# Routing attention and a token/channel mixer on one core: the sums of exponentials taken from one half sum in 14 pairs, and the rounded channel weights stored in rows of 1792 bytes

## The chip, the core and the metric

The kernel runs on one core of a Trainium2 chip. Its engines work side by side and are ordered only by semaphores: TensorE multiplies matrices and writes to PSUM, VectorE and ScalarE do elementwise work and read PSUM, GpSimd does elementwise work between SBUF tiles and can issue transfers of its own, SyncE issues most of the transfers. In the profile they are called PE (PEld for its weight loads), DVE, ACT, POOL and SP. Sixteen DMA engines carry all transfers.

The metric is the time of one execution on the device in microseconds (us). Lower is better.

## What is computed

The inputs are in double precision. Per batch `b` and head `h` the reference gives each query and each key the cluster whose normalised centroid it fits best, and lets a query attend only to the keys of its own cluster. The heads put side by side are the input `x` of an MLP mixer with a token step and a channel step.

```python
q_assign = argmax(q_n @ c_n.T); k_assign = argmax(k_n @ c_n.T)   # 16 clusters per head
scores = where(q_assign == k_assign, q @ k.T / sqrt(64), -1e9)   # 768 x 768
attn = exp(scores - max); attn = attn / (sum(attn) + 1e-9)       # per query
x = concat over heads of attn @ v                                # (4, 768, 512)
u = x + (relu(x.T @ w_tok1) @ w_tok2).T                          # 768 -> 256 -> 768
out = u + relu(u @ w_ch1) @ w_ch2                                # 512 -> 1536 -> 512
```

There are 4 batches, 8 heads, 768 tokens and 64 channels per head.

## The kernel before

**Attention.** The 32 heads are worked as 16 pairs (`NP`), two heads at a time, by `pair(m)`. `scores(m)` issues 12 chunks of score products on TensorE, with a small second product that adds the mask, into PSUM banks 0 to 5 (chunk `n` uses banks `2*(n%3)` and the next one). ScalarE takes the exponential of each chunk (line 1191) into six buffers `st[0..5]` of `[128, 2, 768]`, out of a rotation of seven (`exs`). `values(m, i)` multiplies the exponentials with `v` (16 matmuls of 192 columns for each of `i` = 0 to 5, line 1208, into banks 6 and 7).

The divisor of the softmax needs the sum of the exponentials over all keys. VectorE first adds them elementwise: `es[0] = st[0]+st[1]+st[2]` and `es[1] = st[3]+st[4]+st[5]`, four additions of 128x1536 for a pair (line 881 is the helper `tt` that issues all of VectorE's and GpSimd's two-operand work). `sums(m, bk)` then multiplies both half sums with a matrix of ones, four matmuls of 384 columns for each half (also line 1208), into bank 5; this comes just ahead of `values(m, 5)`. `finish_x(m, 5)` is VectorE's closing part of a pair: transpose the sums (line 1250), clip them (1252), take the reciprocal (1259), transpose the values out of banks 6 and 7 into `x` (1264), and multiply (881). Inside the values of pair m lie the four matmuls of `route(m + 2, 0)`, whose result VectorE turns into cluster assignments (lines 1086 to 1091); the mask goes through DRAM (`wdm`) and back.

**Weights.** Beside attention, VectorE rounds the double precision weights to single precision in 31 pieces (`weight_round`, lines 1327 to 1337 and one addition), paced over the attention by planned times. For the channel weights, `channel_weights` loads pieces of two parts with rows of 512 bytes, writes four operands into `O`, forms four more by sums (`sub1`, 256 elements each), forms four combinations of seven operands (`sub2`, 448 elements each), and stores seven blocks per round to DRAM (`wd1`, `wd2`): 12 rounds, 84 stores of 224 KB with rows of 256 bytes.

**Token step and channel step.** Both use a seven-product scheme (sums of operands in place of an eighth product). In the channel step each of the 28 calls of `product` fetches seven blocks of weights of 192 KB from `wd1` or `wd2` into a ring of eight buffers (196 fetches with rows of 1536 bytes), one for three matmuls of 384 columns, and the results are taken out of PSUM by VectorE or ScalarE. In the products with `w_ch1` two sets of three PSUM banks take turns.

**What sets the order.** Every operation is added to a `Program` with its engine(s), a cost in the author's own figures, and what it reads and writes. `Program.plan` lays a schedule from these figures, TensorE in the order in which the work is written down, the others by due time, and the instructions are emitted in that order. On the chip each engine then runs its list in order and waits where a semaphore says so.

Of the kernel before, what the change touches and what calls it, by code (L numbers as in the profile page):

```python
# [9 lines left out]
F32 = mybir.dt.float32  # L10
# [10 lines left out]
P = 128  # L21
NJ = S // P
# [27 lines left out]
GRAIN = 32  # L50

# [668 lines left out]
def kernel(  # L720
# [36 lines left out]
    wd1 = dram.tile([7, 7, P, 3 * P], F32, name="wd1")  # L757
    wd2 = dram.tile([7, 7, P, 3, P], F32, name="wd2")
# [45 lines left out]
    O = buf(119, [8, 2, 2, W])  # L804
# [343 lines left out]
    def scores(m):  # L1148
# [26 lines left out]
        for n in range(2 * NJ):  # L1175
# [57 lines left out]
    def sums(m, bk):  # L1233
        for n in range(2):
# [4 lines left out]
                        tokens(es[n].ap.rearrange("p h t -> p (h t)"), gr), n == 0, n == 1,  # L1239
# [7 lines left out]
    def finish_x(m, bk):  # L1247
        b, hp = divmod(m, H // 2)
        x, rcp = xs[b], rcps[m % 2]
        vec(lambda: nc.vector.transpose(out=denT.ap, in_=ps[:, bk, 0:HS]), 0.57, bank(bk), denT.k())  # L1250
        def den():
# [9 lines left out]
        cols = slice(hp * P, (hp + 1) * P)  # L1261
        xk = x.rows(0, NJ, hp * P, (hp + 1) * P)
        vec(
            lambda: nc.vector.transpose(  # L1264
                out=x.ap[:, :, cols].rearrange("p j (c d) -> p c j d", d=32),
                in_=ps[:, 6:8, 0:HS],
            ),
            0.96, bank(6, 7), xk,
        )
# [13 lines left out]
    def pair(m):  # L1283
# [23 lines left out]
    def weight_round(srcs, dst, wr, perm=None, after=12.0):  # L1307
# [10 lines left out]
        for part, src, w in srcs:  # L1318
            dma(part(raw.ap), src, [], raw.k((2 * c, 2 * (c + w))), w, 512, after)
            c += w  # L1320
# [63 lines left out]
    def channel_weights(which, after):  # L1384
# [3 lines left out]
        for s in range(6):  # L1388
            for K in range(2):
                srcs = []  # L1390
                for kk in range(2):
                    def part(r, kk=kk):
                        r = r.rearrange("p (k c) two -> p k (c two)", k=2)
                        return r[:, kk].rearrange("p (m c) -> p m c", m=4)

                    kq = 2 * K + kk
                    if which == 1:
                        rows = slice(kq * P, (kq + 1) * P)
                        view = moe_w_ch1[rows].bitcast(U32).rearrange(
                            "p (m c) -> p m c", m=4  # L1400
                        )[:, :, 2 * W * s : 2 * W * (s + 1)]
                    else:
                        c, hf = divmod(s, 2)
                        rows = slice(kq * 3 * P + c * P, kq * 3 * P + (c + 1) * P)
# [602 lines left out]
```

## Time and profile before

| | before |
|---|---|
| median of 3 runs | 799.79 us (799.49 to 800.53) |
| the profiled execution | 799.38 us, of which its span is 797.6 us |
| granted TensorE clock | 0.999 |
| busy: TensorE, VectorE, ScalarE, GpSimd | 783.8, 659.4, 469.8, 188.8 us |
| attention, 16 pairs | up to 333 us of the span |
| token step | 333 to about 410 us |
| channel step | from about 409 us to the end |

The page's share of busy time is an average over stages. The windows of the profile give busy time in a stretch, the chain lists the work that ended last in order of time, and the groups by shape give the duration of one instruction. A busy TensorE says only that matmuls were under way. The column "DMA share" is the mean busy share of the 16 DMA engines; it can pass 1 because packets of one engine overlap.

### The profile page before, as it was taken

Reading aid. Unit: us, or ns where it says so; the run is one execution under the profiler, and the core shown is the slowest. Engines: PE = TensorE matmul, PEld = TensorE weight load, DVE = VectorE, ACT = ScalarE, POOL = GpSimd, SP = SyncE. Lnnn points to the kernel's source line nnn. Section 1 sums busy time; section 2 is a strip of 40 time slices with the busy share of each in tenths; the row PEclk is TensorE's granted clock in tenths of the full one; section 3 lists DMA queues with packets and bytes.
Section 4 is the critical chain, followed back from the end, with each engine's and each line's share of the span. In section 5 each row is a group of like instructions: output and inputs, shape, how many; then the busy total and the mean of one; then the engine's idle time right before and its main releaser. Section 6 shows DMA issues by size and latency. Waiting matters only on the chain.

```text
span 797.6 us, 15467 instructions
## 1 busy us (share of the span) xinstructions
PE 783.8 (98%) x6063; PEld 466.9 (59%) x6063; DVE 659.4 (83%) x861; ACT 469.8 (59%) x618; POOL 188.8 (24%) x184
## 2 busy tenths in 40 slices
PE   7999999999999999999999999999999999999997
PEld 5566666666666666544555555555555555555554
DVE  6988899999999999999994677899952566799964
ACT  5588888888888875698714568503256104400433
POOL 0000000000000000000353499800186379840000
PEclk9999999999999999999999999999999999999999
DMA  9466779999999985479848787635597433333766
GB/s 213 153 160 167 172 169 229 223 211 215 229 226 237 223 249 134 97 148 211 177 122 274 270 290 265 223 99 144 143 210 195 130 106 102 99 104 105 177 148 154
DMA packets 264881, 143.69 MB, mean 180 GB/s; under 512 B 184160, under 2 KB 260704, under 8 KB 264800
## 3 DMA queue, kind: packets, MB, share of 16 engines
q1 hardware_dynamic: 262432, 141.83, 70.2%
q8 instruction: 50, 0.82, 0.4%
q10 hardware_dynamic: 2368, 0.79, 0.4%
q14 instruction: 31, 0.25, 0.1%
HBM read 91.95 MB, written 28.61 MB: 151 GB/s over the span
## 4 chain that ended last, share of the span: by engine, by line
PE 82%; DVE 11%; ACT 4%; issue 2%; ACTq 0%; DVEq 0%
PE ps L842 65%; PE ps L1208 17%; DVE arena L881 9%; ACT arena L871 3%; ACT arena L861 1%; ACT arena L888 0%; DVE arena L863 0%; DVE arena L1264 0%; DVE arena L1337 0%; ACTq L901 0%; ACT L980 0%; ACT arena L1191 0%; DVE arena L1334 0%; DVE arena L1331 0%; DVE arena L1086 0%
## 5 line engine op out<-in xcount | busy, mean ns | idle before, releaser
L842 PE MATMUL ps<-arena 128*128 128x384 f32 (+5 forms) x2735 | 639.7, 462 | 8.4 <-DVE arena L881 2.1
L842 PEld LDWEIGHTS ps<-arena 128*128 128x128 f32 (+1 forms) x2351 | 341.1, 184 | 252.0 <-issue 62.7
L881 DVE TENSOR_TENSOR arena<-arena 128x1536 f32<-128x1536 f32 (+6 forms) x341 | 354.8, 1063 | 19.8 <-ACT arena L1191 9.0
L881 POOL TENSOR_TENSOR arena<-arena 128x384 f32<-128x384 f32 x178 | 188.1, 1086 | 516.5 <-DVE arena L881 382.4
L881 DVE TENSOR_TENSOR arena<-ps,arena 128x384 f32<-128x384 f32 (+3 forms) x227 | 189.3, 844 | 100.2 <-PE ps L842 90.4
L871 ACT COPY arena<-arena 128x768 uint16<-128x768 uint16 x223 | 192.0, 952 | 58.7 <-DVE arena L881 29.3
L1191 ACT ACTIVATE arena<-ps 128x768 f32<-128x768 f32 x192 | 153.8, 810 | 30.4 <-PE ps L842 29.3
L1208 PE MATMUL ps<-arena 128*32 128x192 f32 (+1 forms) x3328 | 151.1, 339 | 0.0
L1208 PEld LDWEIGHTS ps<-arena 128*32 128x32 f32 x3328 | 106.5, 110 | 48.0 <-issue 18.3
L861 ACT COPY arena<-ps 128x1152 f32<-128x1152 f32 (+2 forms) x45 | 32.8, 738 | 133.7 <-PE ps L842 125.2
L888 ACT ACTIVATE arena<-arena 128x1152 f32<-128x1152 f32 (+1 forms) x38 | 40.0, 1077 | 55.8 <-DVE arena L881 55.3
L1865 ACT ACTIVATE arena<-arena 128x768 f32<-128x768 f32 x40 | 38.5, 967 | 17.3 <-DMA arena<-in_moe_w_ch_dram 17.0
L842 PEld LDWEIGHTS <-arena 64*128 64x128 bf16 x384 | 19.2, 94 | 25.0 <-issue 0.6
L1095 ACT ACTIVATE arena<-arena 128x384 bf16<-128x384 f32 x16 | 11.3, 707 | 16.3 <-issue 9.9
L1331 DVE SCALAR_TENSOR_TENSOR arena<-arena 128x512 uint32<-128x512 uint32 (+1 forms) x31 | 20.5, 667 | 0.5
L1337 DVE SCALAR_TENSOR_TENSOR arena<-arena 128x512 f32<-128x512 uint32 (+1 forms) x31 | 20.3, 666 | 0.5
L1264 DVE STREAM_TRANSPOSE arena<-ps 128x768 f32<-128x768 f32 x16 | 15.6, 974 | 0.6 <-PE ps L1208 0.4
L1327 DVE TENSOR_SCALAR arena<-arena 128x512 uint32<-128x512 uint32 (+1 forms) x31 | 12.6, 406 | 0.3 <-DMA arena<-in_moe_w_ch_dram 0.3
L1334 DVE TENSOR_SCALAR arena<-arena 128x512 uint32<-128x512 uint32 (+1 forms) x31 | 12.3, 409 | 0.4
L1086 DVE STREAM_TRANSPOSE arena<-ps 128x384 f32<-128x384 f32 x16 | 9.2, 575 | 3.0 <-PE ps L842 2.7
L1250 DVE STREAM_TRANSPOSE arena<-ps 128x384 f32<-128x384 f32 x16 | 9.2, 575 | 0.8 <-PE ps L1208 0.6
L1091 DVE STREAM_TRANSPOSE arena<-arena 128x384 f32<-128x384 f32 x16 | 9.3, 578 | 0.6
(58 smaller groups left out, 47.2 us busy)
## 6 DMA issues: line engine op xcount, KB each, us to landing
arena<-wd SPq DMA_DIRECT2D x196, 192.0 KB, 2.4
wd<-arena SPq DMA_DIRECT2D x84, 224.0 KB, 3.6
arena<-in_moe_w_ch_dram SPq DMA_DIRECT2D x48, 256.0 KB, 4.6
arena<-in_moe_w_ch_dram SPq DMA_DIRECT2D x16, 768.0 KB, 5.3
arena<-in_v_dram SPq DMA_DIRECT2D x16, 384.0 KB, 4.8
out_dram<-arena SPq DMA_DIRECT2D x14, 384.0 KB, 4.1
arena<-in_k_dram SPq DMA_DIRECT2D x13, 384.0 KB, 4.0
arena<-in_q_dram SPq DMA_DIRECT2D x13, 384.0 KB, 4.4
```

Of the source, the lines that this page charges most:

```text
L842: nc.tensor.matmul(dst, lhsT=lhsT, rhs=rhs, start=start, stop=stop, tile_position=pos, is_transpose=tr, skip_group_check=True,)
L861: nc.scalar.copy(out=dst, in_=src)
L871: nc.scalar.copy(out=dst, in_=src)
L881: (nc.vector if e == "DVE" else nc.gpsimd).tensor_tensor(out=dst, in0=a, in1=b, op=op)
L888: nc.scalar.activation(out=dst, in_=src, func=ACT.Relu)
L1191: lambda e, ex=ex, s=s, u=u: nc.scalar.activation(out=ex.ap[:, :, u * HS : (u + 1) * HS], in_=ps[:, 2 * s : 2 * s + 2, 0:HS], func=ACT.Exp ...
L1208: nc.tensor.matmul(dst, lhsT=lhsT, rhs=rhs, start=start, stop=stop, tile_position=pos, skip_group_check=True,)
L1264: lambda: nc.vector.transpose(out=x.ap[:, :, cols].rearrange("p j (c d) -> p c j d", d=32), in_=ps[:, 6:8, 0:HS],),
L1327: vec(lambda: nc.vector.tensor_scalar(out=hh, in0=hi, scalar1=0x07FFFFFF, scalar2=3, op0=ALU.bitwise_and, op1=ALU.logical_shift_left,), f, ...
L1331: vec(lambda: nc.vector.scalar_tensor_tensor(out=TT, in0=hi, scalar=0xC0000000, in1=hh, op0=ALU.bitwise_and, op1=ALU.bitwise_or), 0.14 + 0 ...
L1337: vec(lambda: nc.vector.scalar_tensor_tensor(out=ll, in0=lo, scalar=float(2.0**-52), in1=hh.bitcast(F32), op0=ALU.mult, op1=ALU.mult,), 0. ...
L1865: lambda e, i=i, func=func, bias=bias, n=n, hi=hi: nc.scalar.activation(out=hi, in_=hi, func=func, bias=bias, accum_out=wsum.ap[:, i, n : ...
```

## The change

**Sums.** A string gives each of the 16 pairs a letter, `-VTVTVTVTVTVTVT-`. For the 14 pairs with a letter the second half sum takes in the first, and `sums` multiplies only `es[1]` with the ones (four matmuls in place of eight). For V (pairs 1, 3, ... 13) VectorE does the addition, one more of 128x1536. For T (pairs 2, 4, ... 14) GpSimd issues a transfer from `es[0]` to `es[1]` that adds at its destination (768 KB read, 768 KB added to). Pairs 0 and 15 keep both halves.

**Their place.** `sums(m - 1)` and the closing part that uses it now come after `values(m, 0)` of the next pair, still in bank 5; the additions of pair m are written down behind them. `finish_x` is split: the transpose of the values (part 0) stays at the end of its pair, the rest (part 1) goes with the sums. For pair 15 the sums stay ahead of `values(15, 5)`, in bank 4.

**Weights.** `wd1` and `wd2` become `wds`, stored as `[7, 128, 6, 7, 64]`: a store writes 1792 bytes in one row for each partition (128 rows in place of 896), and a fetch reads 256 bytes per row (768 rows in place of 128). `O` is laid out with the operand index inside, so that a store's source is contiguous, and a piece of weights is loaded by four transfers of 128 KB in place of two of 256 KB, with rows of 512 bytes as before.

```diff
+FOLD = "-VTVTVTVTVTVTVT-"
...
-    wd1 = dram.tile([7, 7, P, 3 * P], F32, name="wd1")
-    wd2 = dram.tile([7, 7, P, 3, P], F32, name="wd2")
+    wds = [dram.tile([7, P, 6, 7, W], F32, name=f"wd{i}") for i in (1, 2)]
...
-    O = buf(119, [8, 2, 2, W])
+    O = buf(119, [2, 2, 8, W])
...
+    def add_up(m):
+        st = unit[m]
         for n in range(2):
             a = es[n]
             x, y, z = st[HJ * n : HJ * n + HJ]
             tt(a.ap, x.ap, y.ap, ALU.add, 2 * S, x.k() + y.k(), a.k())
             tt(a.ap, a.ap, z.ap, ALU.add, 2 * S, a.k() + z.k(), a.k())
+        a, b = es[1], es[0]
+        if FOLD[m] == "V":
+            tt(a.ap, a.ap, b.ap, ALU.add, 2 * S, a.k() + b.k(), a.k())
+        if FOLD[m] != "T":
+            return
+
+        def fn(e):
+            nc.gpsimd.dma_start(
+                a.ap.rearrange("p h t -> p (h t)"), b.ap.rearrange("p h t -> p (h t)"),
+                accum_op=ALU.add,
+            )
+
+        g.add({"POOL": 1.0}, fn, a.k() + b.k(), a.k(), (2.2 * 768 * 1024, 6144))
...
     def sums(m, bk):
-        for n in range(2):
+        first = 0 if FOLD[m] == "-" else 1
+        for n in range(first, 2):
...
-                        tokens(es[n].ap.rearrange("p h t -> p (h t)"), gr), n == 0, n == 1,
+                        tokens(es[n].ap.rearrange("p h t -> p (h t)"), gr), n == first, n == 1,
...
-            if i == NJ - 1:
-                sums(m, 5)
+            if i == 1:
+                if m:
+                    sums(m - 1, 5)
+                    finish_x(m - 1, 5, 1)
+                add_up(m)
+            if i == NJ - 1 and m == NP - 1:
+                sums(m, 4)
             values(m, i)
-        finish_x(m, 5)
+        finish_x(m, 5, 0)
+        if m == NP - 1:
+            finish_x(m, 4, 1)
...
-                dma(d.rearrange("o p c -> p o c"), src, rd, [("wd", which, pn, s)],
-                    224, 4 * W)
+                dma(wds[which - 1][pn, :, s], src, rd, [("wd", which, pn, s)], 224, 28 * W)
...
-            src = wd1[qi, pn] if wide else wd2[qi, pn].rearrange("p a c -> p (a c)")
             dma(
-                w.ap.rearrange("p a c -> p (a c)"), src,
-                [("wd", which, pn, s) for s in range(6)], w.k(), 192, 1536,
+                w.ap.rearrange("p a (b c) -> p (a b) c", c=W), wds[which - 1][pn, :, :, qi],
+                [("wd", which, pn, s) for s in range(6)], w.k(), 192, 256,
             )
```

More of the change, by code (lines that the diff above doesn't have):

```diff
@@ L1317, in weight_round @@
         c = 0
-        for part, src, w in srcs:
-            dma(part(raw.ap), src, [], raw.k((2 * c, 2 * (c + w))), w, 512, after)
+        for part, src, w, *at in srcs:
+            dma(part(raw.ap), src, [], raw.k(*(at or [(2 * c, 2 * (c + w))])), w, 512, after)
             c += w
@@ L1391, in channel_weights @@
                 for kk in range(2):
[L1392 to L1394 removed]
                     kq = 2 * K + kk
                     if which == 1:
[L1398 to L1401, printed above, removed]
+                        w, at = moe_w_ch1[kq * P : (kq + 1) * P], 2 * W * s
```

67 lines of the change are left out of this document (35 added, 32 removed).

## The prediction

> **What bounds the kernel now.** I read the page's busy line first, then windows by stage, then the chain in order of time, then VectorE's groups by shape in the pairs' steady stretch.
>
> ```profile
> PE 783.8 (98%) x6063; PEld 466.9 (59%) x6063; DVE 659.4 (83%) x861; ACT 469.8 (59%) x618; POOL 188.8 (24%) x184
> ```
>
> ```profile
> 117.00:314.60 197.60, 197.60 (x2878) 123.45 (x2880) 190.58 (x276) 161.13 (x206) 0.00 (x0) 1.00 0.92 219
> ...
> 333.00:372.00 39.00, 38.43 (x93) 16.80 (x90) 34.97 (x59) 35.10 (x48) 0.00 (x0) 1.00 0.81 168
> 372.00:410.00 38.00, 36.49 (x109) 19.93 (x109) 37.16 (x75) 22.65 (x27) 13.31 (x13) 1.00 0.75 162
> ```
>
> ```profile
> 166.33 5.34 PE ps L1208 x128
> 171.66 0.65 PE ps L842 x8
> 172.31 3.89 PE ps L1208 x80
> 176.20 9.89 PE ps L842 x72
> ```
>
> The columns of the windows are length, then busy time of PE, PEld, DVE, ACT, POOL, then the granted clock, the DMA share and GB/s. In ten pair periods (117 to 314.6) TensorE is never idle, at full clock, so a period is the sum of its matmuls: scores 9.89, four value groups 5.34, route 0.65, then two value groups and both sums 3.89, in all 19.77 us. What TensorE loses there the kernel loses, as long as VectorE follows, and VectorE has only 197.6 - 190.6 = 7 us to spare (3.5%). In the token step (333 to 410) both are near the full time.
>
> **The change, part by part.** The profiled execution took 799.38 us, 0.41 us under the median of 799.79.
>
> *Four matmuls fewer in 14 pairs.* One value group is 5.34 / 4 = 1.335 us, so the two sums in the row of 3.89 take 3.89 - 2 x 1.335 = 1.22 us, one 0.61 us. 14 x 0.61 = 8.5 us less on TensorE, all on the path: -8.5. The period becomes 19.16 us.
>
> *The sums' new place.* `sums(m-1)` overwrites bank 5 after one value group, and the last score chunk of pair m sits in banks 4 and 5 until ScalarE has taken its exponential.
>
> ```profile
> 164.81 2.43 ACT L1191 ACTIVATE arena<-ps 128x768 f32<-128x768 f32 x3
> ```
>
> The last exponential ends at 164.81 + 2.43 = 167.24. The values begin at 166.33, the first group ends at 167.67, 0.43 us later. I take 0; at worst, with a semaphore as slow as 0.6 us, 0.2 x 14 = 3 us. In return the half sums have a whole period to get ready, so pairs no longer need all additions before their own sixth value group; nothing waited there, so no gain.
>
> *VectorE.* Seven additions of 128x1536 are new.
>
> ```profile
> L881 DVE TENSOR_TENSOR arena<-arena 128x1536 f32<-128x1536 f32 x41 | 71.9, 1756 | 2.5 <-DVE arena L881 0.5
> L881 DVE TENSOR_TENSOR arena<-arena 128x448 f32<-128x448 f32 x33 | 20.0, 617 | 0.0
> L881 DVE TENSOR_TENSOR arena<-arena 128x256 f32<-128x256 f32 x34 | 13.3, 418 | 0.5
> L881 DVE TENSOR_TENSOR arena<-arena 128x512 f32<-128x512 f32 x16 | 10.8, 686 | 0.3
> L1331 DVE SCALAR_TENSOR_TENSOR arena<-arena 128x512 uint32<-128x512 uint32 x16 | 10.8, 683 | 0.1
> L1264 DVE STREAM_TRANSPOSE arena<-ps 128x768 f32<-128x768 f32 x11 | 10.7, 977 | 0.2 <-PE ps L1208 0.2
> L1337 DVE SCALAR_TENSOR_TENSOR arena<-arena 128x512 f32<-128x512 uint32 x16 | 10.5, 676 | 0.1
> L881 DVE TENSOR_TENSOR arena<-arena 128x768 f32<-128x768 f32 x10 | 9.6, 958 | 0.3
> L1327 DVE TENSOR_SCALAR arena<-arena 128x512 uint32<-128x512 uint32 x17 | 7.1, 418 | 0.3 <-DMA arena<-in_moe_w_ch_dram 0.3
> L1334 DVE TENSOR_SCALAR arena<-arena 128x512 uint32<-128x512 uint32 x16 | 6.3, 415 | 0.1
> L1250 DVE STREAM_TRANSPOSE arena<-ps 128x384 f32<-128x384 f32 x10 | 5.7, 575 | 0.6 <-PE ps L1208 0.4
> L1086 DVE STREAM_TRANSPOSE arena<-ps 128x384 f32<-128x384 f32 x9 | 5.2, 578 | 0.3 <-PE ps L842 0.2
> L1091 DVE STREAM_TRANSPOSE arena<-arena 128x384 f32<-128x384 f32 x9 | 5.2, 578 | 0.3
> L881 DVE TENSOR_TENSOR arena<-arena 128x384 f32<-128x384 f32 x9 | 5.0, 558 | 0.3
> L1087 DVE TENSOR_REDUCE arena<-arena 128x24 f32<-128x384 f32 x9 | 5.0, 553 | 0.3
> L1259 DVE RECIPROCAL arena<-arena 128x12 f32<-128x12 f32 x10 | 2.3, 228 | 0.3
> L1252 DVE TENSOR_SCALAR arena<-arena 128x12 f32<-128x12 f32 x10 | 1.7, 174 | 0.3
> ```
>
> The order of the changed program moves weight work out of this stretch. Between the same ten closing transposes it has 46 large additions (41 before) and one more multiplication of 768, but 24 additions of 448 (33), 28 of 256 (33), 13 of 512 (16), and 13 rounds of the four bit operations (17 and three times 16). That is +5 x 1.756 + 0.958 - 9 x 0.617 - 5 x 0.418 - 3 x 0.686 - 4 x 0.418 - 3 x (0.683 + 0.415 + 0.676) = -6.9 us. So 190.6 - 6.9 = 183.7 busy in 10 x 19.16 = 191.6 us, 96%, as now: VectorE still follows. Within two periods a V pair is over (its 5 additions) and a T pair under the mean; V's three additions behind the sums' transpose hold back the route's transpose (L1086), which frees bank 0 for the next scores, to some 0.5 us ahead of need. I take 0, with 0 to 0.3 x 7 = 2 us.
>
> What is deferred shows up later. Between the last two closing transposes the new order has more work: about one round, one addition each of 448, 512 and 256, a transpose and a clip, less one multiplication: 4.1 us.
>
> ```profile
> 313.96 0.98 DVE L1264 STREAM_TRANSPOSE arena<-ps 128x768 f32<-128x768 f32 x1 [0.17 <-PE ps L1208]
> ...
> 334.55 0.94 DVE L1264 STREAM_TRANSPOSE arena<-ps 128x768 f32<-128x768 f32 x1
> ```
>
> ```profile
> 332.95 28.59 PE L842 MATMUL ps<-arena 128*128 128x512 f32 x66
> ```
>
> Now this transpose comes 1.6 us after the values end (332.95); with 20.6 + 4.1 us of work in 19.77 (19.16 and the second sum) it comes about 5 us after, so VectorE enters the token step some 3 us later against TensorE. There it has 39 - 35 = 4 us of idle time up to 372, but hardly any in 372 to 410 (37.2 of 38). Bounds 0 and 3; I take half, +1.5.
>
> The rest, three rounds (6.6 us), 8 additions of 448, 8 of 256 and 4 of 512 (11 us), falls into the first channel products.
>
> ```profile
> 479.89 1.36 DVE L881 TENSOR_TENSOR arena<-ps,arena 128x1152 f32<-128x1152 f32 x1 [0.65 <-PE ps L842]
> 481.82 1.36 DVE L881 TENSOR_TENSOR arena<-ps,arena 128x1152 f32<-128x1152 f32 x1 [0.58 <-PE ps L842]
> ```
>
> There an evacuation of 1.36 us comes every 1.93 us, with 0.58 us free. An inserted operation of 0.62 to 0.69 overruns by at most 0.1, and PE's other set of banks takes that up. Bounds 0 and 25 x 0.1 = 2.5; I take +0.5.
>
> *The accumulating transfer.* GpSimd, idle in attention, issues it after the fourth addition of a T pair; TensorE's sums wait for it a period later, and VectorE's first addition of the next pair waits for it too, since that overwrites `es[0]`. On VectorE this wait decides: all weight work and the next closing part queue behind it. Between the two additions the order has 15 to 19 operations in the seven T pairs; for pair 8, the shortest, 0.575 + 0.578 + 0.553 + 0.558 + 0.578 + 0.174 + 0.228 + 0.977 + 0.958 + 2 x 0.683 + 0.617 + 2 x 0.415 + 0.676 = 8.7 us, the longest 10.3, the mean 9.6. No row shows an accumulating transfer. The nearest:
>
> ```profile
> arena<-wd SPq DMA_DIRECT2D x196, 192.0 KB, 2.4
> ...
> arena<-in_moe_w_ch_dram SPq DMA_DIRECT2D x16, 768.0 KB, 5.3
> ...
> arena<-wdt SPq DMA_DIRECT2D x2, 768.0 KB, 6.3
> ```
>
> Plain 768 KB land after 5.3 us, 6.3 beside attention's traffic: the lower end. Two plain ones behind each other, 12.6, are the upper. From 192 KB in 2.4 and 768 KB in 5.3, the part that grows with the bytes is 2.9 x 768 / 576 = 3.9 us and the fixed one 1.4; reading two streams doubles the first: 1.4 + 7.8 = 9.2 us, my value. It just fits: +0. At 12.6 it costs (12.6 - 9.6) x 7 = +21; being earlier gains nothing. The Trainium skill, "DMA: Bandwidth & Descriptors" (Anatomy of one DMA, SWDGE path), fits a GpSimd transfer by 2.0 us and 436 KB per us: an estimate of 3.8 us for plain 768 KB and 5.6 us with the bytes doubled. By that page the wait costs nothing either and has 4 us to spare; the rows of this trace are slower than its fit.
>
> *Stores and fetches.*
>
> ```profile
> 0.00:20.00 20.00, 15.84 (x111) 11.34 (x113) 13.94 (x51) 10.66 (x18) 0.70 (x6) 1.00 0.94 212
> ...
> 450.00:500.00 50.00, 50.00 (x157) 29.40 (x156) 34.99 (x27) 36.52 (x60) 45.19 (x47) 1.00 0.83 281
> ...
> 650.00:700.00 50.00, 50.00 (x156) 29.39 (x155) 36.63 (x29) 18.07 (x16) 47.14 (x49) 1.00 0.36 102
> ```
>
> At the start, mostly queries and keys in rows of 256 bytes, the engines move 212 GB/s at a share of 0.94: 192 KB (197 thousand bytes) take 0.93 us. From 650 to 700 there are 26 fetches of 192 KB at a share of 0.36, 0.69 us each. So a fetch grows by 0.24 us of transfer, against one every 1.92 us and a ring seven fetches ahead (13 us): hidden. In 450 to 500, the fullest stretch, the share goes from 0.83 to about 0.95; if it ran over there, the ring's 13 us would go first. A store of 224 KB falls from 1.08 to about 0.81 us: 84 x 0.27 = 23 us less for the engines, beside TensorE's work: no gain by itself. The 48 further issues on SP have the same rows in all and no one waits on the issue alone: 0.
>
> Sum: 799.38 - 8.5 + 1.5 + 0.5 = 792.9; against the median, +0.4: 793.3 us. Its own range is 790.3 (all deferred work hidden, a little less waiting) to 797.
>
> **Rivals.**
> - *The accumulating transfer is late.* Below 9.6 us it costs nothing; from there each us costs 7, and at 9.6 + 6.5 / 7 = 10.5 us the gain is gone. At 11.5 us: 793.3 + 1.9 x 7 = 807. For it: attention's engines are at a share of 0.92. Against: the 6.3 row has such traffic in it already.
> - *The transfer engines become attention's bound.*
>
> ```profile
> 176.20:195.96 19.76, 19.76 (x290) 12.34 (x290) 19.04 (x29) 17.14 (x22) 0.00 (x0) 1.00 1.05 217
> ```
>
>   A share of 0.92 of 197.6 us is 182 us. Five accumulating transfers with 7.8 us each add 39, some 57 stores save 15: 206 us, 14 over TensorE's 191.6. Queries, keys and masks would then come late: 793.3 + 14 = 807 us, slower. Against: the share is 1.05 in a pair in which TensorE is not idle, so packet times overlap and the share is no measure of what is left; at 450 to 500 281 GB/s go at 0.83. The Trainium skill, same page (Issuing engines are not separate DMA queues), says that transfers from GpSimd, SP and ACT share the 16 engines; no run here shows it yet.
> - *VectorE lags by more than I take*: all upper bounds together, 2 + 3 + 2.5, in place of my 2: 793.3 + 5.5 = 799, still a little faster or the same.
> - *Fetches starve the channel step*: only if 256-byte rows from the new layout cost more than 1.92 us a fetch, twice the 0.93 shown; at 2.0 us 196 x 0.08 = 16 us more.
>
> **How the numbers follow.** My sum 0.54; late accumulation 0.18 (most of it slower, a little the same or faster); engines as bound 0.12; VectorE's lag 0.12 (two thirds faster); fetches 0.04. About 0.2% (1.6 us) is what can be told from no change. Faster 0.54 + 0.08 + 0.02 = 0.64, same 0.07, slower 0.29. The range leaves out a tenth at each end: 790 to 808.
>
> **What will show it.** Right: TensorE's period in the pairs is 19.16 us without idle time; the chain there is all PE; the 7 transfers land in under 9.6 us; VectorE's wait ahead of the large additions stays near zero. Wrong: VectorE idle on a transfer, TensorE idle ahead of line 842 for banks 0 or 5 or for masks, a channel step longer than now.

## The result, and the profile after

The changed kernel took 803.67 us (median of 5 executions, 803.29 to 804.91) against 799.98 (799.49 to 800.96): ratio 1.005, 95% interval 1.004 to 1.0061. Twelve further executions spread more, 801.71 to 810.91 (median 807.47 against 800.32, ratio 1.007, 1.0042 to 1.0097). It is slower by 0.5 to 0.7%, where faster was forecast. The ratios leave out executions far above a kernel's fastest; several kernels below spread by themselves, so their extremes are given too.

The page's busy line of the changed kernel, and its windows over the same stretches as before (columns as in the prediction):

```profile
PE 781.3 (97%) x5951; PEld 466.1 (58%) x5951; DVE 676.1 (84%) x869; ACT 465.5 (58%) x616; POOL 199.8 (25%) x192
```

```profile
117.00:314.60 197.60, 196.11 (x2824) 124.81 (x2822) 186.67 (x259) 161.37 (x212) 4.31 (x5) 1.00 0.85 219
333.00:372.00 39.00, 36.29 (x87) 16.09 (x86) 33.66 (x56) 38.97 (x54) 0.00 (x0) 1.00 0.72 166
372.00:410.00 38.00, 36.52 (x110) 20.04 (x109) 37.20 (x73) 16.82 (x20) 15.35 (x15) 1.00 0.74 175
450.00:500.00 50.00, 49.29 (x152) 28.56 (x152) 39.94 (x36) 31.42 (x49) 42.49 (x43) 1.00 1.02 286
650.00:700.00 50.00, 50.00 (x157) 29.40 (x156) 35.71 (x27) 16.90 (x15) 47.22 (x49) 1.00 0.45 103
```

TensorE is no longer without idle time in the pairs (196.1 of 197.6), and from 450 to 500 it loses 0.7 us while VectorE works 39.9 us. The granted clock, third column from the right, is 1.00 in all five stretches, but not throughout. Two shorter windows at the start of the channel step show it:

```profile
416.73:418.65 1.92, 0.00 (x1) 0.01 (x1) 1.92 (x3) 0.00 (x0) 1.92 (x3) 1.00 0.57 207
419.29:422.70 3.41, 3.41 (x7) 1.69 (x6) 2.06 (x3) 0.00 (x0) 0.00 (x0) 0.50 0.87 221
```

TensorE has nothing to do for 1.92 us, and 0.64 us later its clock is 0.50 for 3.41 us. Its matmuls of 128x384 start 0.64 us apart there (420.13, 420.77, 421.41) in place of 0.32 (409.15, 409.47, 409.79), so about half of the 3.41, 1.7 us, is lost; this is an estimate, half of TensorE's busy time there. In the profile of the kernel before no idle time of TensorE reaches 1 us, and its clock is 1.00 up to the last matmul.

In an undisturbed period the chain of the changed kernel is all TensorE:

```profile
57.05 9.89 PE ps L842 x72
66.95 5.98 PE ps L1224 x136
72.93 0.65 PE ps L842 x8
73.57 2.60 PE ps L1224 x64
76.17 5.85 PE ps L842 x41
```

A period is 76.17 - 57.05 = 19.12 us, 0.65 less than 19.77: 14 of them are 9.0 us. They were saved, and lost again elsewhere. The table reads five points of each profiled execution against the same points of the kernel before (start of pair 0's values, 24.69; first token matmul after attention, 332.95; end of the first, 43rd and 51st channel evacuation of 128x1152, 412.82, 494.79 and 605.28), in us, minus is earlier. The first 49 evacuations belong to the first half's first channel products, the 51st to those of the second half. "Half clock" is half of TensorE's busy time in stretches with a granted clock of 0.50, added up over the profile. The last column is the time of that execution.

| kernel | pair 0 | attention's end | evac. 1 | evac. 43 | evac. 51 | half clock | time |
|---|---|---|---|---|---|---|---|
| changed | +0.6 | -4.7 | -2.6 | +2.8 | +3.8 | 1.7 | 803.67 |
| e1 layout alone | +0.4 | +0.4 | +1.7 | +1.3 | +1.3 | 0 | 801.04 |
| e2 sums alone | 0.0 | +14.9 | +13.6 | +15.5 | +16.1 | 6.3 | 818.94 |
| e3 transfer alone, 7 pairs | +0.7 | -1.8 | 0.0 | +1.5 | +1.5 | 0 | 801.36 |
| e4 deferral alone | 0.0 | 0.0 | -1.1 | +2.2 | +2.6 | 0 | 802.72 |
| e5 no half sum | 0.0 | +1.1 | +2.7 | +6.0 | +6.0 | 0 | 805.79 |
| e6 earlier clips | +0.6 | +2.5 | +3.5 | +8.9 | +9.5 | 4.6 | 809.67 |
| e7 transfer in 14 pairs | +0.5 | +10.4 | +13.5 | +13.5 | +13.5 | 6.1 | 813.30 |
| e8 as e4, GpSimd's additions cut | +1.0 | +1.0 | -0.6 | -0.9 | -0.5 | 0 | 799.12 |
| e9 changed, once more | +0.7 | +2.2 | +4.4 | +9.8 | +10.4 | 4.7 | 810.51 |
| e10 third buffer | +0.1 | -8.8 | -7.7 | +6.7 | +11.2 | 6.4 | 811.21 |
| e11 before, earlier clips | +0.5 | +0.6 | -1.7 | -2.1 | -1.8 | 0 | 799.40 |
| e12 VectorE's additions alone | +1.1 | -2.3 | -1.5 | +6.2 | +7.1 | 2.8 | 806.57 |
| f1 third buffer, less deferred | 0.0 | -8.9 | -9.1 | +3.6 | +4.3 | 1.7 | 804.07 |
| f2 as f1, transfer in 14 pairs | 0.0 | +3.5 | +4.6 | +5.5 | +6.0 | 4.3 | 806.11 |
| f3 as f1, transfer in 7 pairs | +0.1 | -3.3 | -2.1 | -0.6 | -0.6 | 0 | 799.50 |
| g1 f1, final test later | +0.1 | -8.8 | -8.9 | -6.8 | -6.3 | 0 | 793.45 |
| g2 g1 without clips and step | +1.1 | -7.1 | -5.0 | +2.3 | +10.3 | 4.6 | 809.88 |

For the changed kernel: of 9.0 us attention keeps 5.3 (from +0.6 to -4.7), the token step gives back 2.1, the first channel products 5.4 (1.7 of them by the half clock), the second ones 1.0, and the start and the tail about a half each.

### The profile page after: what moved, and what is told of

Read it like the earlier page. It is cut to its first block, busy times and chain, and to the rows that moved or that the text cites. A ratio compares the mean times of both kernels' runs of the same rounds, so it can differ in the third digit from the quotient of the medians.

```text
span 801.8 us, 15314 instructions
## 1 busy us (share of the span) xinstructions
PE 781.3 (97%) x5951; PEld 466.1 (58%) x5951; DVE 676.1 (84%) x869; ACT 465.5 (58%) x616; POOL 199.8 (25%) x192
## 4 chain that ended last, share of the span: by engine, by line
PE 72%; DVE 14%; ACT 5%; DMA 4%; issue 2%; POOL 1%; SPq 0%; DVEq 0%; POOLq 0%
PE ps L842 59%; PE ps L1224 13%; DVE arena L881 12%; ACT arena L871 4%; POOL arena L881 1%; DMA arena<-wdm 1%; DMA arena<-arena 1%; DMA arena<-in_moe_w_ch_dram 1%; DMA arena<-in_v_dram 1%; ACT arena L861 0%; DVE arena L1364 0%; ACT arena L888 0%; DVE arena L1361 0%; DVE arena L1358 0%; DVE arena L863 0%
## 5 line engine op out<-in xcount | busy, mean ns | idle before, releaser
L881 DVE TENSOR_TENSOR arena<-arena 128x1536 f32<-128x1536 f32 (+6 forms) x347 | 370.8, 1092 | 21.2 <-PE ps L1224 6.3
L881 POOL TENSOR_TENSOR arena<-arena 128x384 f32<-128x384 f32 x179 | 192.9, 1115 | 209.6 <-PE ps L842 121.1
L1191 ACT ACTIVATE arena<-ps 128x768 f32<-128x768 f32 x192 | 151.3, 812 | 34.7 <-PE ps L842 33.1
L1224 PE MATMUL ps<-arena 128*32 128x192 f32 (+1 forms) x3216 | 142.5, 334 | 0.0
L1224 PEld LDWEIGHTS ps<-arena 128*32 128x32 f32 x3216 | 103.0, 110 | 42.7 <-issue 14.9
L861 ACT COPY arena<-ps 128x384 f32<-128x384 f32 (+2 forms) x43 | 31.2, 733 | 120.5 <-PE ps L842 120.4
L1213 POOL DMA_DIRECT2D arena<-arena x7 | 6.2, 884 | 299.7 <-DVE arena L1278 299.7
```

What stands on the lines that cost most here:

```text
L861: nc.scalar.copy(out=dst, in_=src)
L881: (nc.vector if e == "DVE" else nc.gpsimd).tensor_tensor(out=dst, in0=a, in1=b, op=op)
L1191: lambda e, ex=ex, s=s, u=u: nc.scalar.activation(out=ex.ap[:, :, u * HS : (u + 1) * HS], in_=ps[:, 2 * s : 2 * s + 2, 0:HS], func=ACT.Exp ...
L1224: nc.tensor.matmul(dst, lhsT=lhsT, rhs=rhs, start=start, stop=stop, tile_position=pos, skip_group_check=True,)
```

## The experiments

"Before" is the run of the kernel before in the same session; intervals are of 95%.

**Which part costs.** e1 takes all hunks of the weights' layout and none of the sums'; e2 the reverse.

> Edit: only the weights' part of the change (operand order, four-part loads, stores in rows of 1792 bytes, fetches in rows of 256 bytes); the sums are as before. In VectorE's order no round of weights and 2 additions of 448 stand behind the first channel evacuation (before: none). Theory A (the seven additions on VectorE push 3 rounds and 8 additions of 448 behind attention, into the first channel products, where each overruns beside GpSimd's work): the time is that of before, 800, within 1.5 us; the first channel products lose at most 1 us. Theory B (the new layout itself, by its fetches and loads, slows the channel step): the 5.4 us lost in the first channel products of the changed kernel and the 1.0 us in the next step are here too, and the time is 805 to 807.

Measured 801.08 (800.46 to 802.29), before 799.89, ratio 1.0015 (1.0006 to 1.0024): theory A. The layout costs 1.2 us, at the start and in the token step, nothing in the channel step.

> Edit: only the sums' part of the change; weights are laid out as before. In VectorE's order 2 rounds of weights and 8 additions of 448 stand behind the first channel evacuation (3 and 8 in the changed kernel). Theory A (work pushed behind attention by the seven additions): nearly the whole loss of the changed kernel is here, 4 to 5 us in the first channel products, about 2 in the token step, and the time is 802.5 to 804. Theory B (the layout): the loss in the channel step is gone, and the time is 797 to 798.

Measured 798.27 to 819.93, median 807.49, ratio 1.0029 (0.9996 to 1.0062): neither theory. The profiled execution is one of the long ones. Its DMA issues and VectorE's waits in attention (us in total, times, longest):

```profile
arena<-arena POOLq DMA_DIRECT2D x7, 768.0 KB, 10.0
```

```profile
DVE arena L882 <- DMA arena<-arena: 18.2, 5, 9.0
```

With the old stores the accumulating transfers land after 10.0 us in the median and VectorE waits 18 us for them; in the changed kernel, with stores in long rows, they land after 8.3 and it waits 1.4:

```profile
arena<-wd SPq DMA_DIRECT2D x196, 192.0 KB, 3.0
wd<-arena SPq DMA_DIRECT2D x84, 224.0 KB, 3.6
arena<-in_moe_w_ch_dram SPq DMA_DIRECT2D x96, 128.0 KB, 3.5
arena<-in_moe_w_ch_dram SPq DMA_DIRECT2D x16, 768.0 KB, 5.7
arena<-in_v_dram SPq DMA_DIRECT2D x16, 384.0 KB, 5.4
arena<-arena POOLq DMA_DIRECT2D x7, 768.0 KB, 8.3
```

That fits a transfer made late by the stores' many small rows, but this one pair of profiles doesn't prove it.

```diff
-FOLD = "-VTVTVTVTVTVTVT-"
+FOLD = "--T-T-T-T-T-T-T-"      # e3
+FOLD = "-" * 16                # e5
+FOLD = "-V-V-V-V-V-V-V--"      # e12
```

> Edit: the changed kernel with half sums added in the seven pairs of the accumulating transfer alone; the seven pairs of VectorE's additions keep two matmuls for their sums. No round and 4 additions of 448 stand behind the first channel evacuation. TensorE has 7 x 0.61 = 4.3 us less to do. Theory A: VectorE has no work added, so the losses in the token step and the first channel products shrink to 1 us together: 799.8 - 4.3 + 1 = 796.5, between 795.5 and 798.5 (the waits for masks in attention may stay). Theory B: the layout's 6.4 us stay: 802. Theory C (the accumulating transfers disturb attention's loads and VectorE, and cost the 3.9 us that attention fell short of its 8.5): attention gains nothing, and the time is 800 or more.

Measured 802.02 (800.30 to 802.75), ratio 1.0024 (1.0013 to 1.0035): theory C comes nearest by its time, though attention does gain. Attention keeps 2.5 of its 7 x 0.65 = 4.5 us, the token step loses 1.7, and 1.5 more are gone by the seventh evacuation, all without an added operation on VectorE.

> Edit: the changed kernel with no half sums added in any pair; all sums keep two matmuls, in their new place one pair later. No round and 2 additions of 448 are behind the first channel evacuation. Theory A (the new place is free): attention's values end where the layout alone had them, 0.4 us behind the kernel before, and the time is that of the layout alone, 801.1, within 0.7 us. Rival P (the new place itself costs TensorE some 0.2 us in each period, as in the run with the transfer alone, where pairs without an added half took 19.96 in place of 19.77 us): attention's end is 3 us later and the time is 803.5 to 804.5.

Measured 805.84 (805.0 to 806.59), before 800.20, ratio 1.0064 (1.0044 to 1.0083): above rival P's time, and not by its mechanism. Pair 0's sums move into the next pair's time, which puts the next pairs 1.2 us ahead, and between pairs 2 and 13 nearly nothing of that is lost (-1.2 to -0.9). The last pair loses 2.0: pairs 14 and 15 both sum there, and the last sum waits 0.5 for its own additions. Attention ends 1.1 us late. Then 1.5 go in the token step and 3.3 in the first channel products. Against e1 the new place costs 4.8 us by the medians.

**Deferred work.**

```diff
-START, STEP = 14, 11           # kernel before
+START, STEP = 14, 14           # e4
```

> Edit: the kernel before, with the planner's step between due times of the weights' rounds raised from 11 to 14, so that 3 rounds and 8 additions of 448 stand behind the first channel evacuation, as in the changed kernel; no addition, transfer or layout is changed. Theory A: the first channel products lose about 5 us, as in the changed kernel, and the time is 804 to 806, though TensorE's and VectorE's work is that of before. Theory B or C: deferred work is covered by the 0.58 us free in each period, and the time is 800, within 1 us.

Measured 802.90 (802.44 to 808.06), ratio 1.0055 (1.0034 to 1.0075): theory A's way, but under its 804 to 806. Up to attention's end it is the kernel before to 0.01 us. The token step gains 1.1, with the same eight additions of 448 and five rounds on VectorE from 333 to 404 in both: ahead of its additions of 512 VectorE waits 3.0 us for ScalarE's clips in the kernel before, and for none here. Then 3.3 are lost up to the 43rd evacuation, at a clock of 1.00.

```diff
+    x, y, z = (v[:, :, 0:32] if thin else v for v in (dst, a, b))   # thin: GpSimd's, first channel products
```

> Edit: the kernel before with the step of 14 (3 rounds and 8 additions of 448 deferred, as in the run on that alone, 802.9), and GpSimd's operand additions of the first channel products cut to 32 of 384 columns in the same places and order; their other columns are left out, so the products of that step are not the reference's. Theory A1 (deferred operations cost because VectorE's additions between two tiles in SBUF take up to twice as long beside GpSimd, 1.19 in place of 0.61 us for 448 columns): these take 0.62 again, the loss between the seventh and the 37th evacuation goes from 1.7 to under 0.5 us, and the time is 800.5 to 801.7. Rival A2 (they cost by their place in VectorE's queue and by the stores that they wait for): the time stays at 802.5 to 803.3.

Measured 798.69 (797.95 to 800.87), before 800.20, ratio 0.9977 (0.9959 to 0.9995): A1, by more than expected. VectorE's groups from 412 to 510 of the kernel before, of e4 and of e8, one fence each:

```profile
L881 DVE TENSOR_TENSOR arena<-ps,arena 128x1152 f32<-128x1152 f32 x41 | 55.6, 1357 | 30.7 <-PE ps L842 30.1 <-ACT arena L1865 0.6
L881 DVE TENSOR_TENSOR arena<-arena 128x448 f32<-128x448 f32 x4 | 4.6, 1159 | 0.1
...
L1880 DVE SCALAR_TENSOR_TENSOR arena<-arena 128x192 f32<-128x192 f32 x1 | 0.4, 357 | 0.0
...
L1877 DVE TENSOR_SCALAR arena<-arena 128x192 f32<-128x192 f32 x1 | 0.2, 250 | 0.0
```

```profile
L881 DVE TENSOR_TENSOR arena<-ps,arena 128x1152 f32<-128x1152 f32 x41 | 55.4, 1354 | 14.2 <-PE ps L842 13.8
L881 DVE TENSOR_TENSOR arena<-arena 128x448 f32<-128x448 f32 x12 | 11.9, 998 | 0.0
L881 DVE TENSOR_TENSOR arena<-arena 128x256 f32<-128x256 f32 x8 | 4.4, 578 | 0.1
```

```profile
L886 DVE TENSOR_TENSOR arena<-ps,arena 128x1152 f32<-128x1152 f32 x41 | 55.7, 1357 | 16.3 <-PE ps L842 15.9
L886 DVE TENSOR_TENSOR arena<-arena 128x448 f32<-128x448 f32 x11 | 7.5, 693 | 0.0
L886 DVE TENSOR_TENSOR arena<-arena 128x256 f32<-128x256 f32 x8 | 3.1, 419 | 0.1
```

An addition of 448 between two tiles in SBUF takes 1.16 and 1.00 us here, against 0.617 in the pairs; with GpSimd's additions cut it takes 0.69. The evacuations, one operand of which is in PSUM, take 1.36 us in all three. Of e4's loss 0.7 us is one wait of TensorE for GpSimd itself, which e8 takes away too, so not all of the gain need come by VectorE.

**The accumulating transfer.**

```diff
-    es = [buf(84 + 6 * i, [2, S]) for i in range(2)]       # pair m: es[n]
+    es = [buf(kb, [2, S]) for kb in (84, 90, 152)]         # pair m: es[(2 * m + n) % 3]
-    tmps = [[buf(146 + 6 * i + 2 * n, [WMAX], U32) for n in range(3)] for i in range(2)]
+    tmps = [buf(146 + 2 * n, [WMAX], U32) for n in range(3)]          # e10: one scratch set
```

> Edit: the changed kernel with three buffers for the half sums in turn, so that the first two additions of the next pair no longer wait for the accumulating transfer; the memory comes from the second set of the rounding's scratch buffers, which puts 4 rounds and 12 additions of 448 (3 and 8 before) behind the first channel evacuation. Theory W (VectorE's wait for the transfer is what makes the masks late and costs attention some 3 us): no execution loses on masks, attention's values end 6.5 to 7.5 us ahead of the kernel before (4.7 in the changed kernel) and the spread is gone; with 1 to 2 us more lost in the first channel products the time is 802.5 to 804.5. Rival (the transfers hold up the masks' own transfers): mask waits stay, and attention gains 4.7 us or less.

Measured 810.07 (807.58 to 812.19), before 800.32, ratio 1.0111 (1.0075 to 1.0146): theory W in attention, whose end comes 8.8 us early with no wait for masks; the time is 5.6 us above the range I gave, since 19 us go from the first to the 51st evacuation. TensorE stands idle there four times for 1.1 to 4.0 us, 9.0 in all, and three stretches at half clock behind these take 6.4; the deferred work alone is not the cause. In the same stretch of attention as above, TensorE is without idle time again:

```profile
117.00:314.60 197.60, 197.60 (x2852) 124.53 (x2852) 187.49 (x249) 167.99 (x216) 4.31 (x5) 1.00 0.85 211
```

> Edit: none, the changed kernel once more, to see how its time varies beside the run with the earlier clips, whose attention has the same order of instructions up to the last pair and yet ended 7 us later in its profile. Theory V (how late the accumulating transfers land varies from one execution to the next, and VectorE's wait for them and the masks behind it with it): these executions spread as well, over some 801 to 811 us. Rival (the earlier clips did something else): all lie within 803 to 805, as the first five did.

Measured 801.71 to 810.91: theory V. In the first profile of the changed kernel the chain through a late transfer ran so:

```profile
111.22 0.50 DVE arena L1278
111.72 0.04 issue
111.77 9.80 DMA arena<-arena
121.62 0.40 issue
122.02 1.77 DVE arena L881
...
131.41 4.41 DMA arena<-wdm
135.82 0.04 issue
135.86 4.35 PE ps L842 x29
```

It lands after 9.8 us, VectorE's additions follow, behind them the route's mask, its way through DRAM, and TensorE starts late. In the profile of e9 the longest transfer takes 14.0 us, and the same waits of VectorE in attention (1.4 us in the first profile), and what TensorE waits for up to 420 (0.7), are longer:

```profile
DVE arena L881 <- DMA arena<-arena: 6.3, 3, 5.0
```

```profile
PE ps L842 <- DVE arena L1086: 4.1, 2, 3.4
```

Behind the 3.4 us of idle time the clock is 0.50 for 6.83 us (177.08 to 183.91), which takes 3.0 more.

> Edit: the changed kernel with half sums added by VectorE in the seven V pairs and no accumulating transfer; 2 rounds and 8 additions of 448 are behind the first channel evacuation. Theory W (the transfers cost attention its missing gain, the additions do not): no wait for masks; attention's values end 4.3 us ahead of the run with the new place alone, that is 3.2 us ahead of the kernel before, and all executions lie within 2 us; the channel step loses as in the changed kernel or as with the place alone, 5 to 9 us: 802 to 806. Rival (VectorE's additions hold up the route's work, so that TensorE waits in each V pair): attention gains less than 2 us against the place alone.

Measured 805.63 (804.50 to 806.95), ratio 1.0062 (1.0045 to 1.0079): theory W. Attention's end is 3.4 us earlier than in e5 with a start 1.1 later, which is the whole 7 x 0.65 = 4.5, without waits for masks and within 2.5 us in all executions. The 7.7 us that it loses from the first to the 43rd evacuation are nearly all one held operation (last section): 4.7 us in which TensorE is idle behind it, and 2.8 by the half clock after that.

> Edit: the changed kernel with the accumulating transfer in all 14 pairs and no addition on VectorE, the planner's step between rounds of weights 9.5 in place of 11 (no round and no addition of 448 is then behind the first channel evacuation), and the clips as in the run before. TensorE has the full 8.5 us less to do. Theory A (the additions on VectorE and the work they push out are what costs; a transfer that lands in 8 to 9 us is nearly free): against the run with seven transfers and no additions, 802.0, another 4.3 us in attention, 1.5 in the first channel products and 2 in the token step are gained: 794 to 797. Theory C (the transfers are what costs: 14 of them in succession disturb the loads and hold VectorE): the time is 800 or more.

With a step of 9.5 and e6's clips. Measured 819.83 (813.30 to 823.10), ratio 1.0232 (1.0188 to 1.0275): theory C, with two buffers.

```profile
PE ps L842 <- DMA arena<-wdm: 12.8, 4, 5.4
```

**ScalarE's order in the token step.**

```diff
-    relu(d, d, DM, dk, dk, ("ACT",))
+    relu(d, d, DM, dk, dk, ("ACT",), 20.0)      # due 20 us earlier, the eight clips of the token step
```

> Edit: the changed kernel; the eight clips of the token step on ScalarE get due times 20 us earlier in the planner, so that 34 instead of 38 splitting copies stand ahead of the last clip, and 10 instead of 25 ahead of the second. Theory O (the 2.1 us lost in the token step come from ScalarE's order, five more copies of 0.95 us ahead of the last clip than in the kernel before): the token step gains 2 to 4 us and the time is 800 to 801.7. Rival (they come from VectorE's late entry into the token step, as the prediction had it): the time stays at 803.7, within 0.7 us.

Measured 808.85 (800.75 to 814.27), ratio 1.0068 (1.0037 to 1.0099): inconclusive in time, since attention spreads as in e9. By the table the token step loses 1.0 in place of 2.1, and TensorE's wait for a clip there is 1.1 us in place of 1.9.

> Edit: the kernel before, its sums and weights as they were, with the eight clips of the token step due 20 us earlier on ScalarE and a step of 10 between rounds of weights; 27 splitting copies stand ahead of the last clip in place of 33. Theory O (the token step is set by how many copies ScalarE runs ahead of its clips): 6 copies of 0.95 us less, of which the chain behind VectorE gives back about half: 2 to 4 us gained, 796 to 798. Rival: VectorE bounds the token step (37.2 of 38 us busy) and the time is 799.5 to 800.5.

Measured 799.50 (798.93 to 807.45), ratio 0.9994 (0.9971 to 1.0018): not told from no change. The step is 10 here besides, so two edits act at once. The token step did gain 2.3 us, as theory O has it, and 1.8 of it lasted to the 51st evacuation; its span is that of the kernel before, 797.6, and what takes the rest at the end is not shown.

**All causes together.** f1 to f3 take memory for the third buffer from one of three load buffers and one shared scratch buffer.

```diff
+    raws = [buf(134 + 4 * i, [WMAX, 2], U32) for i in range(2)]
+    tmps = [[buf(k, [WMAX], U32) for k in (142 + 4 * i, 144 + 4 * i, 150)] for i in range(2)]
```

> Edit: the changed kernel with three buffers for the half sums in turn, their memory from one of three load buffers and one shared scratch buffer (both rounding sets stay), clips due 20 us earlier, a step of 9 between rounds; 2 rounds and 8 additions of 448 deferred. Theory: attention's values end 8 to 8.8 us ahead of the kernel before, the token step keeps that, the channel step loses 6 to 8 by the deferred work: 798 to 801, with executions within 3 us of each other. Rival (two load buffers make the rounds wait for their loads, or more work slips behind): 803 or more.

Measured in two groups, five executions at 793.89 to 795.20 and seven at 804.07 to 806.04, ratio 0.9987 (0.995 to 1.0024): the theory's 798 to 801 lies between them. The granted clock parts the groups too, 0.998 to 0.999 in the first and 0.992 to 0.995 in the second. The profiled one is of the second group. Its timeline (start, length; GpSimd's row groups 28 instructions without a gap):

```profile
447.16 26.87 POOL L881 TENSOR_TENSOR arena<-arena 128x384 f32<-128x384 f32 x28 [2.26 <-DVE arena L881]
...
464.42 9.84 DVE L1901 SCALAR_TENSOR_TENSOR arena<-arena 128x192 f32<-128x192 f32 x1
```

Line 1901 is the second operation of the final test of the sums, with two operands in SBUF. It takes 0.36 us in the kernel before (L1880 above); here it stands from 464.42 to 474.26 and ends with GpSimd's run (447.16 + 26.87 = 474.03), and the evacuations queue behind it. TensorE is idle for 8.6 us, from 466.98 to 475.58, and then short of clock:

```profile
472.21:479.04 6.83, 3.46 (x6) 1.95 (x7) 4.84 (x4) 3.12 (x3) 1.83 (x2) 0.50 0.01 2
```

Half of the 3.46 us is 1.7, and with the 8.6 that is the 10 us between the groups.

> Edit: as the run before, with the accumulating transfer in all 14 pairs and no addition on VectorE; no round and 5 additions of 448 deferred. Theory (the wait and the deferred work are the two causes): attention gains 8 to 8.8 us, the channel step loses 2 to 4: 794 to 798, faster than both kernels. Rival (14 transfers in succession load the engines so that masks and loads come late, as where all 14 pairs used the transfer with two buffers, 12.8 us of mask waits): attention gains under 4 us, the time is 800 or more.

Measured 799.09 (795.82 to 806.11), ratio 0.9983 (0.997 to 0.9996): between the two. In the profiled execution, the longest of all, masks still come late (7.1 us in four waits), with all 14 pairs on the transfer, and the half clock takes 4.3.

> Edit: as the run before, with the accumulating transfer in seven pairs; no round and 2 additions of 448 deferred. Theory: attention gains 4.3 less 0.6 at the start, 3.5 to 4.3 us; the channel step loses 0 to 2: 797 to 799. Rival: as with the place alone the channel step loses 3 to 5 by the planner's order whatever is deferred: 800 or more.

Measured 804.94 (798.48 to 821.60), ratio 1.0034 (1.0008 to 1.006). Its profiled execution, 799.50, goes nearly as the theory had it, most others don't. The granted clock falls as the time grows, from 0.998 at 798.48 to 0.986 at 821.60, so idle times of TensorE with half clock behind them are likely; what TensorE waits for there, no profile shows.

```diff
+    vec(..., 0.3, rd, okb.k(), after=540.0)     # the final test's first two operations, on f1
```

> Edit: as f1_VT (three buffers, earlier clips, step of 9), with the first two operations of the final check, 128x192 in SBUF, held back until all 41 evacuations of the first channel products are done; in f1_VT they stand behind 17 and 23 of them, beside GpSimd's longest run of additions. Theory (such an operation waits until GpSimd's run of additions has a gap, 9.84 us in f1_VT's profile, with the evacuations queued behind it): the slow executions at 804 to 806 are gone and all lie at 793.5 to 796. Rival (another cause): the times stay in two groups 10 us apart.

Measured 793.15 (792.91 to 794.32, 5 executions), before 799.95, ratio 0.9907 (0.9874 to 0.994): the second group is gone, the clock is 0.997 to 0.999 in all five, and this version of the change beats both kernels.

```profile
PE 776.1 (98%) x5951; PEld 463.2 (59%) x5951; DVE 672.5 (85%) x867; ACT 469.5 (59%) x617; POOL 199.3 (25%) x193
```

> Edit: the changed kernel with the three buffers (two load buffers, one shared scratch) and the check's two operations held back, clips and step as in the changed kernel; 2 rounds and 8 additions of 448 deferred, 38 copies ahead of the last clip (32 in g1_check_later). Theory: attention gains 8 to 9 us as in f1_VT, the token step gives back 1 to 3 more than there: 795 to 798.5, still faster than the kernel before. Rival: without the earlier clips the gain is lost to the token step and the channel step: 799 or more.

Measured 805.94 (804.03 to 809.88), ratio 1.0065 (1.0044 to 1.0086): the rival. Attention's gain holds (-7.1 with a start 1.1 later), but with the step of 11 again 7.3 us go up to the 43rd evacuation, 1.7 of them by the half clock, and 8 more up to the 51st: 4.0 behind a fetch of weights that landed 7.1 us after its issue, and 2.9 by the half clock after that.

```profile
PE ps L842 <- DMA arena<-wd: 4.0, 1, 4.0
```

Clips and step were taken out together, so their shares are not parted.

## Why the prediction was wrong

From the profiled 799.38 us the sum gave 792.9, and the profiled execution of the changed kernel took 803.67, 10.8 more. The first channel products make 4.9 of that, the accumulating transfer 3.7, the second channel products 1.0, the token step 0.6, the start and the tail 1.0; the matmuls gained 0.5 more than forecast. The terms one by one:

*Four matmuls fewer in 14 pairs, -8.5.* Right; 19.12 us in place of 19.16, 9.0 us in all, and with a third buffer all of it stays in attention (e10, f1, g1).

*The sums' new place, 0.* Right for bank 5 and the steady pairs, wrong for the rest: e5 ends attention 1.1 us late, by its last pair, and loses 4.8 in later stages, which the working left out. That the planner's new order does it is argued; the wait for a clip (1.6 us) is the part that a row shows.

*VectorE in the V pairs, 0.* Right: in e12 each of them gains 0.6 us and attention waits for no mask.

*The accumulating transfer, 9.2 us, "it just fits: +0".* The size was near (8.3 in the median, 9.8 in the longest of the first profile, 14.0 in that of e9), the step failed at its threshold. A mean of 9.6 us of work between two additions was weighed against one duration; the landing varies, the pairs differ (8.7 in the shortest), and each lateness passes through VectorE's queue to the masks of a later pair. Attention fell 3.7 us short of 9.0 in the first profile (1.5 of them in TensorE's waits for masks, the rest in smaller losses that no row names) and 10.6 in that of e9 (+0.7 to +2.2), 3.0 of them by the half clock. With a third buffer the shortfall is gone (e10). That is the first rival, and in the first profile it is milder. The estimate from the Trainium skill's "DMA: Bandwidth & Descriptors" (3.8 to 5.6 us) was further off; the trace decides.

*Deferred work in the token step, +1.5.* The size was about right (2.1), the reason not: e1 and e3 lose 1.3 and 1.7 there with no addition on VectorE, and e4, with as much work on VectorE, gains 1.1. What tracks the loss is a wait of TensorE for a clip on ScalarE: none in the kernel before and in e4, 1.4 us in e1, 1.5 in e3, 1.6 in e5, and in the changed kernel

```profile
PE ps L842 <- ACT arena L888: 1.9, 1, 1.9
```

By the order of the programs ScalarE runs 38 splitting copies ahead of the last clip, 33 in the kernel before. The ends of these chains, before and after:

```profile
365.27 1.64 ACT arena L871 x2
366.90 0.54 ACT arena L888
367.44 0.02 issue
367.47 1.30 DVE arena L881 x2
```

```profile
368.29 0.93 ACT arena L871
369.22 0.47 ACT arena L888
369.69 0.04 issue
369.73 8.65 PE ps L842 x26
```

e11 and e6 give part of it back when the clips are due earlier, so the order is a cause, and the clip's lateness stands for 1.9 of the 2.1 us; how much of that the five copies make is not settled.

*Deferred work in the first channel products, +0.5 (0 to 2.5).* This is the largest of the steps that failed: 5.4 us, without which the changed kernel would have come out 1 us faster. "An inserted operation of 0.62 to 0.69 overruns by at most 0.1" took durations from attention, where GpSimd is idle. Beside GpSimd's additions they take 1.00 to 1.16 us in the mean, and then fill more than the 0.58 us free. It also took them one by one between evacuations, while the new order puts a round and three additions of 448 ahead of the first evacuation that VectorE takes; two of the three take 2.75 us in the changed kernel (414.58 to 417.33), and TensorE waits 1.9 us for that evacuation. e4 shows the cost without any part of the change (3.3 us, after e4's token step had gained 1.1), e8 that it goes when GpSimd's additions shrink. The other 1.7 us are the half clock behind the idle 1.9; the working had no term for it, and e4, idle for 1.7 us at the same place, kept its clock. The row was in the trace of before: four additions of 448 in that very stretch at 1159 ns, shown above. The Trainium skill, "SBUF — State Buffer" (Who interferes with whom), says that a VectorE instruction with two inputs in SBUF contends with GpSimd's reads and that one with at most one, outside its two-port modes, doesn't; the 1.16 us against the unmoved 1.36 agree.

*Stores and fetches, 0.* Right for the changed kernel: a fetch grew from 2.4 to 3.0 us and nothing waited for it. In e10 and g2 TensorE did wait for one, 2.0 and 4.0 us. The rival that the engines become the bound did not come true.

With the losses taken away by edits (a buffer, the order, the final test later), g1 takes 793.15 us, where 793.3 was forecast. That the two agree is luck in part: g1 loses nothing in the token step and 2.1 us in the first channel products, where the sum had 1.5 and 0.5, its attention keeps 8.9 in place of 8.5, and its settings are not those of the forecast.

## What to carry to other kernels

Price an operation that moves into another stage by rows of that stage, above all where another engine works beside it there. Where a transfer is to fit into a gap, set the shortest gap against the longest landing and say who queues behind; a further buffer made the difference here. An idle time of TensorE can cost more than its length: look for a lower granted clock in windows of a few microseconds behind it, which a mean over a long stretch blurs. In a program whose order a planner makes, read the new order of every engine, not of the one that the edit touches.

## What the runs showed of the hardware

In f1's profile a VectorE operation between tiles in SBUF was held up for 9.84 us (0.36 alone) until GpSimd's run of 28 additions ended. In e12's a `tensor_scalar` of 128x192 took 5.88 us (0.25 alone), to the end of such a run:

```profile
454.54 26.91 POOL L881 TENSOR_TENSOR arena<-arena 128x384 f32<-128x384 f32 x28
...
475.69 5.88 DVE L1898 TENSOR_SCALAR arena<-arena 128x192 f32<-128x192 f32 x1
```

The Trainium skill, same page and section, says of VectorE's two-port modes that whoever issues first holds the shared ports for the whole instruction and the other blocks; no run here shows in which mode an operation ran. Most stretched operations would fit one such instruction, with up to 0.8 us more; one GpSimd addition takes 26.87 / 28 = 0.96 us, so these two were held for several. The shorter executions of f1 leave no room for it, and in its profile the operation before it (line 1898) passed beside the same run in 0.28 us; what decides it was not tried.

In all these profiles together the granted clock is 0.50 in 20 stretches ahead of the last matmul, of 3.41 or 6.83 us each and 1.00 elsewhere. Each began within 5.3 us of the start of an idle time of TensorE of 1.89 us or more. Of the 24 such idle times 20 had one behind them and four, of 2.2 to 3.4 us, had none; none of the idle times up to 1.86 us had one by itself. So of two idle times near 2 us one can cost 1.7 us more and the other nothing (1.92 us in the changed kernel, 2.22 in f3); the length does not settle it alone, and what else does was not tried.

An accumulating transfer of 768 KB from SBUF to SBUF landed after 6.7 us (e10) to 10.0 us (e2) in the median.
